# Attention backward on one core: query-major exponentials 384 keys wide, the fourth key tile by DMA transposes

## The chip, the cores and the metric

The kernel runs on one core of a Trainium2 chip. A core has TensorE (PE; its weight loads are listed as PEld), VectorE (DVE), ScalarE (ACT), GpSimd (POOL) and SyncE (SP), which here only issues DMAs. The metric is device time in microseconds, the median of three runs.

## The reference, cut to what matters

A layer of two branches, forward and backward. Branch A is attention over 2048 tokens with 32 heads of width 18; branch B is a long convolution with a state-space kernel; a gate mixes them. The stage in question is the attention with its gradients:

```python
qkv = (x @ wqkv).reshape(B, S, 3, H, Dh)          # S = 2048, D = 576, H = 32, Dh = 18
scores = einsum("bhqd,bhkd->bhqk", q, k) * Dh ** -0.5
p = softmax(scores, axis=-1)
o = einsum("bhqk,bhkd->bhqd", p, v)
a = o.reshape(B, S, D) @ wo
# and the gradients: dv = p^T do, ds = p * (do v^T - rowsum(do * o)), dq = ds k, dk = ds^T q
out = g * a + (1 - g) * b                          # with jax.vjp of the whole for grad_out
```

## The kernel before, in words

Four heads form a group; there are 8 groups (NG). A unit is one group and one block of 512 queries (b), so there are 32 units (NU), and each is worked in 32 steps (NST). All engines' work is written out by hand in one loop over the global step G, in the order in which each engine runs it; nothing is reordered afterwards, and the waits between engines are put in from the tiles' uses. The backward half of a unit runs OFF = 39 steps behind its forward half, so in steps 39 to 1023 both halves run, of neighbouring units.

What one step does, in this order on TensorE:

- P1: a pair of score matmuls of two heads, key-major (128 keys of tile i by 512 queries), into a PSUM tile `ps_P`. ScalarE takes the exponential into a stored tile `PT` (128 x 1024, bf16, L1388), out of a ring of 41 such tiles. `PT` is kept until the backward half of the unit uses it.
- a burst of the slot of this step: dV, dQ or dK, each in two halves (`dv_half`, `dq_half`, `dk_half`), or transposes by TensorE (`turn_p`). All share one PSUM buffer (`accB`), which DVE evicts (L1151, L1169, L1188, L1102). A key block (kq) of 512 keys takes eight steps.
- P3: the same scores once more for the backward half, query-major (128 queries of tile ii by 512 keys), with a second exponential into `eb` (L1393). dV needs the probabilities with the queries on the partitions, since a matmul sums over partitions. The key-major `PT` is what the forward output and ds need.
- P2: two matmuls of dO and V with two PSUM buffers, from which DVE makes ds by multiplying with `PT` (L1398).
- in half of the steps, the forward output `accO` from `PT`.

Scores thus are exponentiated twice, once in each layout. P1 and P3 use two score buffers in turn, P2 two of its own.

dK needs ds with keys and queries exchanged (`dsT`). Three of the four heads of a tile of ds are turned by a DMA transpose, issued on SP as soon as DVE has made them (L1406), the fourth by TensorE; two pairs of tiles in a unit are done otherwise (`by_pe`). SP also issues, in program order, the loads of the next pieces (`QaT`, `KaT`, `VaT`, and by DMA transposes `Vtok`, `Ktok`, `Qtok`) and the transposes of finished gradients (`gT`). When a group ends, eight `gT` for dK and dV and four `Ktok` and four `VaT` of the next group come within about one unit: this is called a change of group below; there are seven in the stretch where both halves run.

At the end of a unit's forward half, `post_forward` evicts `accO` (DVE, `oT`), turns it on TensorE, takes reciprocals (`rl`, DVE), and POOL multiplies: `dOa` from `rl` (L1049) and `prod` from it (L1051), which DVE then reduces (L1057). POOL's other work during attention is the basis of branch B (L506, stored by L559), written between the steps at an even rate (`e_emit`), and packing of gradients (`dtk`, L1075, stored by L1076). POOL also works strictly in the order written.

After the last step the next stage (branch B) begins; its first loads are issued on SP during the last 39 steps, in which only the backward half runs.

Line numbers here and in the profile are those of the kernel before; the same code lies some lines further down in the kernel after (L1406 becomes L1427, L1010 becomes L1012, L1071 becomes L1073).

## Time and profile before

| what | value |
|---|---|
| median of 3 runs | 2677.37 us (2671.75 to 2682.45) |
| span of the profiled execution | 2673.6 us |
| TensorE clock granted, mean | 0.968 |
| busy over the span: PE, DVE, ACT, POOL | 90%, 86%, 88%, 68% |
| exponentials, key-major (L1388) | x1024, record 1075 ns each |
| exponentials, query-major (L1393) | x1024, record 1070 ns each |
| products ds (L1398) | x2048, record 683 ns each |
| DMA transposes of ds (L1406) | x512 |
| queue q1 (SP) | 1108346 packets, 339.13 MB |

The profiled execution is given by its span alone, which lies 3.8 us under the median of the runs. The attention stage reaches from the first score matmul at 120.6 us to the last product at 2086.6 us. A record of an instruction on ScalarE or DVE is longer than its distance to the next one, since neighbours overlap; the pace is read from start to start. The DMA share is the sum of packet times over 16 engines and can exceed 1.

### The profile page before, as it was taken

What the parts mean: (1) busy time and instruction counts of PE and PEld (TensorE: products, weight loads), DVE (VectorE), ACT (ScalarE), POOL (GpSimd) and SP (SyncE); (2) the same over time, 40 slices, a digit from 0 to 9 for tenths busy, and PEclk for the clock granted to TensorE, in tenths of its full rate; (3) what the DMA queues carried; (4) which work ended last, traced back from release to release, by engine and by line L of the source; (5) the groups of instructions that cost most, each with busy time, mean ns of one, the idle gap of its engine ahead of it and who ended that gap; (6) DMA issues with size and microseconds to landing.
All of it is one profiled execution on the core that took longest, in us unless ns stands there. A gap on an engine that the chain in (4) does not pass through costs nothing.

```text
span 2673.6 us, 69952 instructions
## 1 busy us (share of the span) xinstructions
PE 2405.5 (90%) x27411; PEld 1134.6 (42%) x27411; DVE 2294.7 (86%) x4090; ACT 2352.0 (88%) x2744; POOL 1830.1 (68%) x2845
## 2 busy tenths in 40 slices
PE   8999999998889898889898999989988699999999
PEld 4433333333333333333333333333232489998756
DVE  5748999999889999889899999999897499999964
ACT  5589999999999999999999999999996489999321
POOL 0388878888888888888878888887931135555431
PEclk9989999999999999999999999999896699999999
DMA  7747889879979978997898899779668979998996
GB/s 232 202 114 152 150 171 177 162 156 181 169 151 172 185 157 163 173 167 152 165 179 157 157 172 169 154 164 181 134 136 174 224 229 262 260 263 250 269 255 136
DMA packets 1155478, 486.63 MB, mean 182 GB/s; under 512 B 1071062, under 2 KB 1108551, under 8 KB 1152843
## 3 DMA queue, kind: packets, MB, share of 16 engines
q1 hardware_dynamic: 1108346, 339.13, 64.3%
q0 software_dynamic: 44784, 137.52, 19.2%
q10 hardware_dynamic: 2016, 5.51, 0.7%
q8 instruction: 214, 3.51, 0.6%
q14 instruction: 118, 0.96, 0.1%
HBM read 146.27 MB, written 93.80 MB: 90 GB/s over the span
## 4 chain that ended last, share of the span: by engine, by line
ACT 39%; PE 28%; DVE 22%; issue 6%; DMA 3%; POOL 2%; SPq 1%; ACTq 0%; DVEq 0%; POOLq 0%
ACT eb L1393 23%; ACT PT L1388 14%; PE ps_P L30 8%; DVE ds L1398 7%; DVE tz L733 3%; DVE wab L753 3%; PE accV L30 2%; PE ps_dx L30 2%; PE turn_p L1097 2%; DVE tz L736 2%; PE accK L30 2%; DVE HG L738 2%; PE yp L30 2%; DVE Rw L758 1%; DVE dvacc L1151 1%
## 5 line engine op out<-in xcount | busy, mean ns | idle before, releaser
L1398 DVE TENSOR_TENSOR ds<-ps_P,PT 128x512 bf16<-128x512 f32 x2048 | 1312.5, 683 | 127.8 <-PE ps_P L30 87.3
L1393 ACT ACTIVATE eb<-ps_P 128x1024 bf16<-128x1024 f32 x1024 | 1095.7, 1070 | 44.3 <-PE ps_P L30 44.2
L1388 ACT ACTIVATE PT<-ps_P 128x1024 bf16<-128x1024 f32 x1024 | 1099.6, 1075 | 11.0 <-PE ps_P L30 9.5
L30 PE MATMUL ps_P<-dOaT,VaT_g 32*128 32x512 bf16 x2048 | 583.1, 390 | 30.8 <-DVE ds L1398 15.4
L506 POOL TENSOR_TENSOR et<-eG,eT 128x448 f32<-128x448 f32 x576 | 542.9, 963 | 10.7
L30 PE MATMUL ps_P<-QaT_g,KaT_g 32*128 32x512 bf16 x2048 | 404.7, 387 | 126.6 <-ACT PT L1388 122.2
L30 PE MATMUL ps_P<-KaT_g,QaT_g 32*128 32x512 bf16 x2048 | 408.9, 392 | 2.0 <-ACT eb L1393 1.4
L506 POOL TENSOR_TENSOR Eo<-et,et 128x448 bf16<-128x448 f32 x288 | 327.2, 1136 | 20.8
L30 PEld LDWEIGHTS <-KaT_g 32*128 32x128 bf16 x2048 | 147.4, 91 | 456.1 <-issue 438.2
L30 PEld LDWEIGHTS <-QaT_g 32*128 32x128 bf16 x2048 | 115.7, 91 | 288.6 <-issue 266.7
L30 PE MATMUL accV<-eb,dOa 128*32 128x512 bf16 x2048 | 185.6, 396 | 26.8 <-ACT eb L1393 26.5
L30 PE MATMUL accO<-PT,Vtok_g 128*32 128x512 bf16 x2048 | 207.9, 395 | 0.1
L30 PE MATMUL accK<-dsT,Qtok_g 128*32 128x256 bf16 x4096 | 165.3, 283 | 21.3 <-DMA dsT<-ds 19.9
L30 PE MATMUL accQ<-ds,Ktok_g 128*32 128x512 bf16 x2048 | 161.9, 394 | 2.2 <-DVE dvacc L1151 1.9
L30 PEld LDWEIGHTS <-Vtok_g 128*32 128x32 bf16 x2048 | 52.8, 93 | 222.6 <-issue 222.6
L1102 DVE COPY dsT<-turn_p 128x1024 bf16<-128x1024 bf16 (+1 forms) x216 | 139.2, 644 | 3.4 <-PE turn_p L1097 3.4
L1097 PE MATMUL turn_p<-ident_bf,ds 128*128 128x128 bf16 x1664 | 136.2, 225 | 1.4 <-DVE gb L1169 0.8
L672 ACT COPY E1e<-etp 128x1024 bf16<-128x1024 bf16 x132 | 125.4, 1063 | 2.7 <-PE etp L671 2.7
L30 PEld LDWEIGHTS <-Qtok_g 128*32 128x32 bf16 x4096 | 88.6, 97 | 87.8 <-issue 57.9
L506 POOL TENSOR_TENSOR et<-eT 128x32 f32<-128x32 f32 (+3 forms) x288 | 116.2, 424 | 11.4
L1097 PEld LDWEIGHTS <-ds 128*128 128x128 bf16 x1664 | 98.9, 100 | 50.2 <-issue 50.0
L1075 POOL COPY dtk<-gT 128x288 bf16<-128x288 bf16 x96 | 40.9, 426 | 107.6 <-DMA dqkv_d<-dtk 47.2
(295 smaller groups left out, 3731.0 us busy)
## 6 DMA issues: line engine op xcount, KB each, us to landing
E_d<-Eo POOLq DMA_DIRECT2D x144, 256.0 KB, 3.3
E1n<-E_d POOLq DMA_DIRECT2D x30, 1024.0 KB, 6.6
T0w<-Kp_d SPq DMA_DIRECT2D x18, 1024.0 KB
xs<-xb_d POOLq DMA_DIRECT2D x28, 512.0 KB, 9.9
dsT<-ds SPq DMA_TRANSPOSE x512
dqkv_d<-dtk POOLq DMA_DIRECT2D x96, 72.0 KB, 4.3
Md_d<-mst SPq DMA_DIRECT2D x18, 288.0 KB
skw<-Md_d SPq DMA_DIRECT2D x72, 64.0 KB
```

Of the source, the lines that this page charges most:

```text
L30: return nc.tensor.matmul(out, lhsT=lhsT, rhs=rhs, start=start, stop=stop, **kw)
L506: nc.gpsimd.tensor_tensor(out, a, b, op=op)
L672: copy(E_[:, 4 * q:4 * q + 4], pt_)
L733: nc.vector.tensor_tensor(tz[x], HG[:, :, k - 1].unsqueeze(1).to_broadcast([P, 2, 2, n, CB]), ZZ.unsqueeze(3).to_broadcast([P, 2, 2, n, CB ...
L736: nc.vector.tensor_tensor(tz[x][:, 0], tz[x][:, 0], UVk[:, :, :, k, :], op=A.add)
L738: nc.vector.tensor_tensor(HG[:, :, k], tz[x][:, 0], tz[x][:, 1, ::-1], op=A.add)
L753: nc.vector.tensor_tensor(wab, h_, w_, op=A.mult)
L1097: nc.tensor.transpose(pt_[:, x, qb, :], t_[:, qb * P:(qb + 1) * P], ident_bf)
L1102: (nc.scalar.copy if NTOT <= now[0] < NTOT + OFF else nc.vector.tensor_copy)(o_(), pt_[:, x:x + n])
L1388: nc.scalar.activation(U["PT"][i, j // 2], ps, ACT.Exp)
L1393: nc.scalar.activation(e, ps, ACT.Exp)
L1398: nc.vector.tensor_tensor(U["ds"][i][:, j, :], ps, U["PT"][i, j // 2][:, j % 2, :], op=A.mult)
```

## The change

Query-major scores and exponentials now cover only the first 384 keys of each block of 512 (KT = KB - P). For the fourth key tile of each block, the stored key-major tiles `PT` of both head pairs are turned by a DMA transpose on SP into `PTt` (two buffers), and dV of these 128 keys is made from `PTt`: in each half burst, eight matmuls of 384 columns and eight of 128 in place of eight of 512. The transposes of a block are issued one and two steps after the block's first backward step, five or six steps ahead of its dV burst. The `eb` tiles shrink to 2 x 384; the number of all other tiles stays.

```diff
-        woT = [eds.tile([P, 2, 512], BF, tag="eb", bufs=8, name="eb")...
-        dO_st = [eds.tile([P, 2, 512], BF, tag="eb", bufs=8, name="eb") for _ in range(3)]
+        woT = [eds.tile([P, 2, 384], BF, tag="eb", bufs=8, name="eb")...
+        dO_st = [eds.tile([P, 2, 384], BF, tag="eb", bufs=8, name="eb") for _ in range(3)]
...
+            KT = KB - P
+            TURNED = (0, 1)
...
+                def turn_p(u, kq, pair):
+                    U = UN[u]
+                    t_ = U["PTt", kq, pair] = work.tile([P, 2 * TPQ, P], BF, tag="PTt", bufs=2, name="PTt")
+                    nc.sync.dma_start_transpose(out=t_, in_=U["PT"][kq * TPQ + 3, pair].rearrange("p x q -> p (x q)"))
...
                 def dv_half(g, b, kq, h, acc):
                     U = UN[(g, b)]
-                    for ii in (2 * h, 2 * h + 1):
+
+                    def stored(ii):
                         for j in range(4):
-                            mm(acc[HP * j:HP * (j + 1), :], lhsT=U["dOa"][:, ii, j, :], rhs=U["eb"].pop((kq, ii, j)),
+                            mm(acc[HP * j:HP * (j + 1), 0:KT], lhsT=U["dOa"][:, ii, j, :], rhs=U["eb"].pop((kq, ii, j)),
                                start=(ii == 0), stop=(ii == 3), tile_position=(0, HP * j))
+
+                    def turned(ii):
+                        for j in range(4):
+                            mm(acc[HP * j:HP * (j + 1), KT:KB], lhsT=U["dOa"][:, ii, j, :], rhs=U["PTt", kq, j // 2][:, j % 2 * TPQ + ii, :],
+                               start=False, stop=False, tile_position=(0, HP * j))
+                    stored(2 * h)
+                    turned(2 * h)
+                    turned(2 * h + 1)
+                    stored(2 * h + 1)
...
+                for u_ in range(NU):
+                    for kq_ in range(NQ):
+                        for x_, pair_ in enumerate(TURNED):
+                            at(("pre", u_ * NST + OFF + 8 * kq_ + 1 + x_), lambda u_=u_, kq_=kq_, pair_=pair_: turn_p(units[u_], kq_, pair_))
...
-                            row(ps[:, x, :], T["QaT", b][:, ii * P:(ii + 1) * P], T["KaT", kq], jo + x)
+                            row(ps[:, x, 0:KT], T["QaT", b][:, ii * P:(ii + 1) * P], T["KaT", kq][:, 0:KT], jo + x)
...
-                            e = eds.tile([P, 2, KB], BF, tag="eb", bufs=8, name="eb")
+                            e = eds.tile([P, 2, KT], BF, tag="eb", bufs=8, name="eb")
...
-                            nc.scalar.activation(e, ps, ACT.Exp)
+                            nc.scalar.activation(e, ps[:, :, 0:KT], ACT.Exp)
```

Instructions issued on SP rise by the 256 transposes (two for each of 4 key blocks of 32 units), those of TensorE by 2048 matmuls with their weight loads; ScalarE, DVE and POOL issue the same ones as before.

More of the change, by code (lines that the diff above doesn't have):

```diff
@@ L125, in build @@
         d_aT = [eds.tile([P, 4, 512], BF, tag="ds", bufs=5, name="ds") for _ in range(DC)]
-        woT = [eds.tile([P, 2, 512], BF, tag="eb", bufs=8, name="eb").rearrange("p a b -> p (a b)")[:, 0:D] for _ in range(DC)]
-        dO_st = [eds.tile([P, 2, 512], BF, tag="eb", bufs=8, name="eb") for _ in range(3)]
+        woT = [eds.tile([P, 2, 384], BF, tag="eb", bufs=8, name="eb").rearrange("p a b -> p (a b)")[:, 0:D] for _ in range(DC)]
+        dO_st = [eds.tile([P, 2, 384], BF, tag="eb", bufs=8, name="eb") for _ in range(3)]
         with ExitStack() as ctx:
```

## Prediction

> **What bounds the kernel now.** I read the page's busy shares and 40 slices first, then stretches of equal length inside the attention stage, then the timeline engine by engine. The page says that three engines are nearly full over the span, and POOL not far behind:

> ```profile
> PE 2405.5 (90%) x27411; PEld 1134.6 (42%) x27411; DVE 2294.7 (86%) x4090; ACT 2352.0 (88%) x2744; POOL 1830.1 (68%) x2845
> ```

> Key-major and query-major scores run side by side in 985 of the 1024 steps, from 172 to 2000 us. Two stretches of 59 us there, about one unit (32 steps) each, the second at a change of head group:

> ```profile
> core 0: us, PE busy (x) PEld busy (x) DVE busy (x) ACT busy (x) POOL busy (x), PEclk, DMA share, GB/s
> 1259.00:1318.00 59.00, 53.12 (x580) 18.56 (x576) 53.45 (x90) 59.00 (x66) 49.83 (x78) 1.00 0.78 154
> 1318.00:1377.00 59.00, 53.37 (x580) 18.66 (x577) 53.55 (x89) 59.00 (x66) 47.25 (x78) 1.00 1.03 185
> ```

> The columns are busy us and instructions of PE, PEld, DVE, ACT and POOL, then clock, DMA share, GB/s. ACT is busy all 59.00 us of both, so ScalarE sets the pace. The DMA share goes from 0.78 to 1.03 between them and the pace does not move: that share, above 1, is no ceiling.

> ScalarE's records overlap, so the pace is read from start to start:

> ```profile
> 1008.92 1.07 ACT L1388 ACTIVATE PT<-ps_P 128x1024 bf16<-128x1024 f32 x1
> 1009.83 1.08 ACT L1393 ACTIVATE eb<-ps_P 128x1024 bf16<-128x1024 f32 x1
> 1010.73 1.09 ACT L1388 ACTIVATE PT<-ps_P 128x1024 bf16<-128x1024 f32 x1
> 2167.66 2.10 ACT L708 ACTIVATE UV<-uvp 128x512 bf16<-128x512 f32 x4
> 2169.59 1.06 ACT L743 CAST gR<-HG 128x960 bf16<-128x960 f32 x1
> ```

> A 128x1024 exponential costs 0.905 us (1008.92 to 1010.73 is two), not the 1.07 of its record. Four 128x512 ones cost 1.93, so 0.483 each. Between them lies 0.824 ns per column.

> What the other engines have in hand is POOL's story. Once a unit POOL must turn `rl` into `dOa` and `prod` before DVE can go on (L1049, L1051), between basis operations that it does in the order they were written:

> ```profile
> POOL dOa L1049 <- DVE rl L1044: 92.4, 25, 8.3
> POOL dtk L1075 <- DMA dqkv_d<-dtk: 34.6, 18, 5.6
> 1293.08 0.68 POOL L1049 TENSOR_TENSOR dOa<-dO_b,rl 128x288 bf16<-128x288 bf16 x1 [4.91 <-DVE rl L1044]
> 1411.01 0.68 POOL L1049 TENSOR_TENSOR dOa<-dO_b,rl 128x288 bf16<-128x288 bf16 x1
> ```

> Those two rows are two units apart: 117.93 us, 58.97 a unit. At 1293 POOL had waited 4.91 us for DVE, so it had that much to spare; at 1411, behind a change of group, it had nothing. Over the stretch its spare time at this point is 92.4 us.

> **The change, part by part.** *Exponentials.* 256 columns fewer on each of 985 is 256 x 0.824 ns = 0.211 us a step, 208 us in all, if nothing else bound. A unit of ScalarE would fall to 32 x (0.905 + 0.694) = 51.2 us.

> *DVE* loses nothing:

> ```profile
> 1008.18 1.28 DVE L1398 TENSOR_TENSOR ds<-ps_P,PT 128x512 bf16<-128x512 f32 x2
> 1009.37 0.68 DVE L1102 COPY dsT<-turn_p 128x1024 bf16<-128x1024 bf16 x1
> 1009.97 1.28 DVE L1398 TENSOR_TENSOR ds<-ps_P,PT 128x512 bf16<-128x512 f32 x2
> ```

> From 1008.18 to 1009.37 are two products, 0.595 each; the 128x1024 copy behind takes 0.60. A unit has 64 products, 12 evictions (dV, dQ, dK per key block), some 6.5 such copies and `oT`, 83.5 at 0.60 = 50.1, and about 1.5 of small ones: 51.6 us. So DVE stands where ScalarE will: two engines at 51 to 52.

> *TensorE.* The score matmul of 384 columns runs beside the P2 pair of 512, so nothing is gained there. The dV burst gets 16 more matmuls per key block, with 16 weight loads. First half of one burst, TensorE, before and after (`eb`: query-major tiles, `PTt`: turned key-major ones):

> ```order
> L30 MATMUL accV_2128<-eb_1980,dOa0_1232 32x512
> ...
> L30 MATMUL accV_2128<-eb_1954,dOa0_1232 32x512
> ...
> L30 MATMUL accV_2128<-eb_2033,dOa0_1232 32x512
> ...
> L30 MATMUL accV_2128<-eb_2007,dOa0_1232 32x512
> ...
> L30 MATMUL ps_P3_2138<-KaT_g_1247,QaT_g_1245 128x512
> ```

> ```order
> L30 MATMUL accV_2132<-eb_1982,dOa0_1232 32x384
> ...
> L30 MATMUL accV_2132<-eb_1954,dOa0_1232 32x384
> ...
> L30 MATMUL accV_2132<-PTt_1964,dOa0_1232 32x128
> ...
> L30 MATMUL accV_2132<-PTt_1997,dOa0_1232 32x128
> ...
> L30 MATMUL accV_2132<-eb_2037,dOa0_1232 32x384
> ```

> The turned keys stand between the stored pieces; the columns in all are the same. Eight matmuls and sixteen with as many columns took

> ```profile
> 1001.46 0.62 PE L30 MATMUL accV<-eb,dOa 128*32 128x512 bf16 x8
> 1010.36 0.62 PE L30 MATMUL accK<-dsT,Qtok_g 128*32 128x256 bf16 x16
> L30 PE MATMUL ps_P<-QaT_g,KaT_g 32*128 32x512 bf16 x2048 | 404.7, 387 | 126.6 <-ACT PT L1388 122.2
> ```

> 0.62 both, so the extra instructions cost nothing that shows, and at most a tenth of that, 0.06 us a half, which two rows of equal length would still hide (I take 0). The cover is the third row: TensorE waits 122.2 us for ScalarE to free the score buffer. Were that gone, 0.06 x 246 halves = 15 us.

> *SP, the transposes.* 256 DMA transposes of 8x128 go onto the queue that already issues `dsT`, in order, each `dsT` waiting for DVE. Prices, min/median/max ns:

> ```profile
> L1406 SPq DMA_TRANSPOSE dsT<-ds x512: 1274/1458/5387, 175.8 to 2098.6; - x171
> L1010 SPq DMA_TRANSPOSE Ktok_g<-QKV_d x32: 1225/1262/2299, 158.9 to 1851.5; - x32
> ```

> `dsT` is 12x128 at 1.46, `Ktok` 4x128 at 1.26, so I put 8x128 between, at 1.36; the far end is 2.20 (below). The same place on SP at a change of head group:

> ```order
> L1406 DMA_TRANSPOSE dsT_24063<-ds_24028 128x12x128
> L1010 DMA_TRANSPOSE Qtok_g_24066<-QKV_d_72 128x4x128
> L1071 DMA_TRANSPOSE gT_24068<-dvacc_20631 128x4x128
> L1010 DMA_TRANSPOSE Ktok_g_24102<-QKV_d_72 128x4x128
> L1406 DMA_TRANSPOSE dsT_24063<-ds_24093 128x12x128
> ```

> ```order
> L1116 DMA_TRANSPOSE PTt_25595<-PT_24336 128x8x128
> L1427 DMA_TRANSPOSE dsT_25625<-ds_25588 128x12x128
> L1012 DMA_TRANSPOSE Qtok_g_25628<-QKV_d_72 128x4x128
> L1116 DMA_TRANSPOSE PTt_25630<-PT_24376 128x8x128
> L1073 DMA_TRANSPOSE gT_25632<-dvacc_21951 128x4x128
> L1012 DMA_TRANSPOSE Ktok_g_25666<-QKV_d_72 128x4x128
> L1427 DMA_TRANSPOSE dsT_25625<-ds_25657 128x12x128
> ```

> One `PTt` now stands ahead of the first `dsT`, one ahead of the second. Each waits on SP for the dV burst that frees its buffer, a step earlier; behind it stands a `dsT` whose products come later still, so that wait costs nothing. dV itself wants the `PTt` five or six steps (9 us) after issue. In the trace of before that place reads

> ```profile
> 1329.04 2.20 SPq L1071 DMA_TRANSPOSE gT<-dkacc  x1
> 1331.34 4.13 SPq L1406 DMA_TRANSPOSE dsT<-ds  x2
> 1335.52 1.26 SPq L1010 DMA_TRANSPOSE Qtok_g<-QKV_d  x1
> 1336.89 1.31 SPq L1071 DMA_TRANSPOSE gT<-dvacc  x1
> 1338.25 1.27 SPq L1010 DMA_TRANSPOSE Ktok_g<-QKV_d  x1
> 1339.62 4.58 SPq L1406 DMA_TRANSPOSE dsT<-ds  x2
> ...
> 1346.26 6.12 SPq L1406 DMA_TRANSPOSE dsT<-ds  x2
> ```

> Each row starts where the last ends; SP idles only inside the pairs of `dsT`, 4.13 - 2.92 and 4.58 - 2.92, 2.9 us in the 14.92 of a key block. Two `PTt` take 2.8. So SP is just full there and a unit at a change of group stays at 4 x 14.92 = 59.7. In the other 24 units SP issues 16 x 1.46 + 8 x 1.36 + 3 x 1.26 and some 4 us of plain loads and gaps, 42 us: hidden.

> What a late `dsT` does, the trace has once:

> ```profile
> 1132.01 1.05 PE L30 MATMUL accK<-dsT,Qtok_g 128*32 128x256 bf16 x16 [1.85 <-DMA dsT<-ds]
> 1133.63 1.02 ACT L1393 ACTIVATE eb<-ps_P 128x1024 bf16<-128x1024 f32 x1 [2.14 <-PE ps_P L30]
> 1000.00:1100.00 100.00, 90.05 (x975) 31.14 (x971) 90.11 (x149) 100.00 (x109) 89.18 (x148) 1.00 0.86 163
> 1100.00:1200.00 100.00, 89.05 (x950) 30.91 (x949) 87.99 (x146) 97.12 (x106) 80.95 (x124) 0.97 0.98 173
> ```

> dK waited 1.85 us, ScalarE 2.14, and the clock fell (0.97 over 100 us). ScalarE did 106 instructions instead of 109.5: 3.5 x 0.905 = 3.2 us lost. [...]

> *The tail*, 2000 to 2116, where no exponential bounds. SP is solid there and `dsT` dear, and the stage behind waits for SP's last load:

> ```profile
> 2068.41 2.98 SPq L1406 DMA_TRANSPOSE dsT<-ds  x1
> 2088.01 4.24 SPq L1406 DMA_TRANSPOSE dsT<-ds  x1
> 2103.55 1.12 ACT L603 ACTIVATE RX<-RXn,l1col 128x480 bf16<-128x480 bf16 x1 [16.64 <-DMA E1n<-E_d]
> ```

> Four `PTt` (last two key blocks) fall into it, 1.4 to 4 us each; at 2, since they are half the size of those rows, 8 us lost.

> *Sum.* POOL lets through at most its 92.4 us. 3 of them lie in the seven units at changes of group, which stay; its longest wait, 8.3, is where it runs out of work and DVE and ScalarE allow some 5. That leaves 86. SP takes 0.7 x 7 = 5 and, I take, three more stalls at 3.2 = 10; the tail 8. 86 - 5 - 10 - 8 = 63 of the profiled 2673.6: 2610.6. The median of the runs lies 3.8 above this span, so **2614**. An ordinary unit then takes 55.5 us, all from POOL's spare time, and ScalarE idles 3 to 4 us in it.

> **Rivals.** *POOL gives way.* If its late `dOa` only eats the step or so that DVE leaves before the reduction, ordinary units go to 53, a little above 51.6: 6 x 24 = 143, less 23: 2557. Against it: at 1411 POOL was already on time with nothing left.

> *The ring of P2 and product binds.* With no key-major work left, the query-major score pairs start at

> ```profile
> 2002.51 0.39 PE L30 MATMUL ps_P<-KaT_g,QaT_g 32*128 32x512 bf16 x2
> 2004.22 0.39 PE L30 MATMUL ps_P<-KaT_g,QaT_g 32*128 32x512 bf16 x2
> 2006.17 0.39 PE L30 MATMUL ps_P<-KaT_g,QaT_g 32*128 32x512 bf16 x2
> 2007.99 0.52 PE L30 MATMUL ps_P<-KaT_g,QaT_g 32*128 32x512 bf16 x2
> ```

> 1.71, 1.95 and 1.82 apart, mean 1.83, 58.5 us a unit: nothing saved but 0.5 x 31 = 15, less 23, so 2685, no change. Against it: these three steps hold `oT`, `rl` and `Ob` of a unit's end.

> *SP becomes the bound* (slower). If at changes of group a `dsT` right behind a `PTt` costs what `gT` cost at 1329, 2.20, and each `PTt` 1.9 (as far above its 1.36), the unit takes 16 x 2.2 + 8 x 1.9 + 13 x 1.26 + 6 = 72.8 us, 13.8 more, seven times 97; with 16 in the tail, 2673.6 - 86 + 97 + 16 + 3.8 = 2704. It turns slower where such a unit passes 58.97 + (86 - 8)/7 = 70. For it: stalls of this kind exist. Against: most `dsT` cost 1.46. That the DMA engines themselves fill I count here; against it speaks that they can move more:

> ```profile
> 1001.00:1002.00 1.00, 1.00 (x11) 0.22 (x9) 1.00 (x3) 1.00 (x2) 0.97 (x3) 1.00 1.23 283
> ```

> 283 GB/s while only transposes ran, against 154 and 185 above; 256 x 256 KB in 1.75 ms adds 38.

> **Chances.** Forecast 0.60, POOL gives way 0.14, ring 0.14, SP 0.12. The range reaches both outer rivals, 2557 and 2704: 2555 to 2705. A run tells about 0.5% (13 us). Faster is the forecast nearly whole and the first rival, 0.71; same 0.16; slower 0.13.

> **What would show it.** Right: exponentials of `eb` 0.69 apart, ScalarE idle in ordinary units, POOL's wait before `dOa` near 0, DVE waiting for `prod`, units at changes of group at 59 to 61 with `dsT` waits of TensorE. Wrong: ordinary units at 53 or 58, `dsT` issues above 2 us, half clock outside the stalls, or dV waiting for `PTt`.

## The result

The changed kernel is slower: 2746.42 us median (2732.61 to 2752.76, 4 runs) against 2676.62 (2671.75 to 2682.45, 4 runs), a ratio of 1.0249 with a 95% interval of 1.0208 to 1.0291. The profiled execution has a span of 2751.0 us, 77.4 more than the 2673.6 before. The forecast was 2614, and its range ended at 2705.

The page, where it answers to the rows of before: first the granted clock in 40 slices and the shares of the chain that ended last in the kernel before, then busy time of the engines, clock and chain in the changed kernel.

```profile
PEclk9989999999999999999999999999896699999999
ACT 39%; PE 28%; DVE 22%; issue 6%; DMA 3%; POOL 2%; SPq 1%; ACTq 0%; DVEq 0%; POOLq 0%
...
PE 2505.4 (91%) x29459; PEld 1181.9 (43%) x29459; DVE 2280.3 (83%) x4090; ACT 2200.9 (80%) x2744; POOL 1830.5 (67%) x2845
PEclk9999998897798798978989997998998599999999
PE 55%; DVE 25%; DMA 11%; ACT 4%; issue 3%; SPq 1%; POOL 0%; ACTq 0%; DVEq 0%; POOLq 0%
PE ps_P L30 20%; DVE ds L1419 11%; PE accV L30 7%; DMA PTt<-PT 6%; PE accK L30 5%; PE accQ L30 5%; PE accO L30 5%; DMA dsT<-ds 4%; DVE tz L733 2%; DVE wab L753 2%; PE ps_dx L30 2%; PE ps_proj L30 2%; DVE tz L736 2%; PE ps_dwq L30 1%; DVE HG
```

ScalarE went from 2352.0 us busy to 2200.9: the 151 us less of work are there. TensorE went from 2405.5 to 2505.4 although only narrow matmuls were added, and the clock row, full before in the attention stage up to its end, dips to 7 and 8 all along it. In the chain ScalarE fell from 39% to 4%; it now holds `PTt<-PT` with 6% and `dsT<-ds` with 4%.

A unit at a time tells more. In the attention stage, cut at every 32nd key-major exponential, the units 1 to 30 add up to 1781.8 us before and to 1854.2 after. An ordinary unit before, then two neighbouring units after, the second at a change of head group (columns as before: us, busy of PE, PEld, DVE, ACT, POOL, clock, DMA share, GB/s):

```profile
1190.00:1248.92 58.92, 53.03 (x576) 18.55 (x576) 53.37 (x89) 58.92 (x66) 49.87 (x82) 1.00 0.74 163
...
1320.03:1376.56 56.53, 53.09 (x648) 19.32 (x640) 52.70 (x89) 53.84 (x65) 49.68 (x79) 1.00 1.07 197
1376.56:1441.60 65.04, 60.60 (x648) 20.27 (x640) 53.17 (x89) 54.88 (x65) 51.04 (x84) 0.82 1.10 194
```

The undisturbed unit is 56.53 us, and seven of the 30 lie within 0.1 us of that; it was 58.92. The next one has the same numbers of instructions, but took 65.04, with TensorE busy 60.60 instead of 53.09 at a clock of 0.82. So the change has two effects that nearly hide each other in the total: 30 x (58.92 - 56.53) = 72 us gained, and 1854.2 - 30 x 56.53 = 158 us spent above the undisturbed pace, where before it was 14. The units at a change of group are 68.3 us on average, those right behind them 63.3, the rest 58.3.

What TensorE waited for in the stage after (us in all, times, longest):

```profile
PE accV L30 <- DMA PTt<-PT: 30.9, 27, 6.0
PE accK L30 <- DMA dsT<-ds: 26.4, 15, 4.7
```

dV and dK waited 57 us, in 42 waits; before, dK waited 2.1 us in two. (The expectations below speak of 74 us, with the 16.4 that weight loads waited for `dsT`; laid over dK's waits, all but 4.5 us of these are the same time.) The 57 us are two fifths of the 144 that were lost. The rest goes with the half clock, which follows such waits, but other gaps of TensorE too, as the run without transposes below shows (208 us of half clock, with 9.1 us of such waits). One wait, on SP and on TensorE:

```profile
400.64 1.39 SPq L1116 DMA_TRANSPOSE PTt<-PT  x1
402.12 1.56 SPq L1073 DMA_TRANSPOSE gT<-dvacc  x1
403.74 1.26 SPq L1012 DMA_TRANSPOSE Ktok_g<-QKV_d  x1
405.09 2.46 SPq L1427 DMA_TRANSPOSE dsT<-ds  x1
...
408.28 1.56 SPq L1427 DMA_TRANSPOSE dsT<-ds  x1
...
411.05 1.23 SPq L1073 DMA_TRANSPOSE gT<-dkacc  x1
412.37 2.86 SPq L1427 DMA_TRANSPOSE dsT<-ds  x1
...
416.91 0.39 PE L30 MATMUL ps_P<-QaT_g,KaT_g 32*128 32x512 bf16 x2
418.13 0.62 PE L30 MATMUL accK<-dsT,Qtok_g 128*32 128x256 bf16 x16 [0.83 <-DMA dsT<-ds]
...
421.25 0.63 PE L30 MATMUL ps_P<-QaT_g,KaT_g 32*128 32x512 bf16 x2
...
419.50:443.40 23.90, 23.56 (x200) 7.46 (x198) 16.40 (x26) 17.37 (x21) 18.00 (x38) 0.50 1.09 180
```

dK's wait names the two `dsT` issued at 408.28 and 412.37. By the trace the last product that the second needs ended at 406.60, but SP, still busy with what stands ahead, was through with its issue only at 415.22. dK then waits 0.83 us, and from 419.5 to 443.4 the granted clock is 0.50: two score matmuls that took 0.39 us take 0.63. In these 23.90 us ScalarE did 21 instructions; at the undisturbed pace (65 in 56.53) it would have done 27.5. The 6.5 missing ones are 5.6 us lost behind a wait of 0.83.

### The profile page after: what moved, and what is told of

Read it like the earlier page. It is cut to its first block, busy times and chain, and to the rows that moved or that the text cites. A ratio compares the mean times of both kernels' runs of the same rounds, so it can differ in the third digit from the quotient of the medians.

```text
span 2751.0 us, 74632 instructions
## 1 busy us (share of the span) xinstructions
PE 2505.4 (91%) x29459; PEld 1181.9 (43%) x29459; DVE 2280.3 (83%) x4090; ACT 2200.9 (80%) x2744; POOL 1830.5 (67%) x2845
## 4 chain that ended last, share of the span: by engine, by line
PE 55%; DVE 25%; DMA 11%; ACT 4%; issue 3%; SPq 1%; POOL 0%; ACTq 0%; DVEq 0%; POOLq 0%
PE ps_P L30 20%; DVE ds L1419 11%; PE accV L30 7%; DMA PTt<-PT 6%; PE accK L30 5%; PE accQ L30 5%; PE accO L30 5%; DMA dsT<-ds 4%; DVE tz L733 2%; DVE wab L753 2%; PE ps_dx L30 2%; PE ps_proj L30 2%; DVE tz L736 2%; PE ps_dwq L30 1%; DVE HG L738 1%
## 5 line engine op out<-in xcount | busy, mean ns | idle before, releaser
L1419 DVE TENSOR_TENSOR ds<-ps_P,PT 128x512 bf16<-128x512 f32 x2048 | 1304.8, 683 | 177.3 <-PE ps_P L30 158.9
L1409 ACT ACTIVATE PT<-ps_P 128x1024 bf16<-128x1024 f32 x1024 | 1053.1, 1029 | 100.8 <-PE ps_P L30 80.8
L1414 ACT ACTIVATE eb<-ps_P 128x768 bf16<-128x768 f32 x1024 | 835.7, 816 | 179.3 <-PE ps_P L30 172.6
L30 PE MATMUL ps_P<-dOaT,VaT_g 32*128 32x512 bf16 x2048 | 647.3, 414 | 58.3 <-DVE ds L1419 45.9
L30 PE MATMUL ps_P<-QaT_g,KaT_g 32*128 32x512 bf16 x2048 | 451.9, 414 | 25.9 <-ACT PT L1409 25.0
L30 PE MATMUL ps_P<-KaT_g,QaT_g 32*128 32x384 bf16 x2048 | 371.2, 359 | 1.2 <-ACT PT L1409 0.5
L30 PEld LDWEIGHTS <-KaT_g 32*128 32x128 bf16 x2048 | 130.3, 92 | 328.6 <-issue 304.4
L30 PE MATMUL accO<-PT,Vtok_g 128*32 128x512 bf16 x2048 | 222.0, 423 | 0.1
L30 PE MATMUL accK<-dsT,Qtok_g 128*32 128x256 bf16 x4096 | 177.5, 299 | 47.9 <-DMA dsT<-ds 44.4
L30 PEld LDWEIGHTS <-QaT_g 32*128 32x128 bf16 x2048 | 98.3, 92 | 282.3 <-issue 263.3
L30 PE MATMUL accV<-eb,dOa 128*32 128x384 bf16 x2048 | 189.8, 366 | 6.8 <-ACT eb L1414 6.3
L30 PE MATMUL accQ<-ds,Ktok_g 128*32 128x512 bf16 x2048 | 175.3, 423 | 1.7 <-DVE dvacc L1168 1.7
L30 PEld LDWEIGHTS <-dOa 128*32 128x32 bf16 x4096 | 88.1, 100 | 182.0 <-issue 165.7
L30 PEld LDWEIGHTS <-Vtok_g 128*32 128x32 bf16 x2048 | 53.4, 94 | 258.8 <-issue 258.4
L30 PEld LDWEIGHTS <-Qtok_g 128*32 128x32 bf16 x4096 | 99.6, 101 | 127.5 <-issue 80.0
```

What stands on the lines that cost most here:

```text
L30: return nc.tensor.matmul(out, lhsT=lhsT, rhs=rhs, start=start, stop=stop, **kw)
L1409: nc.scalar.activation(U["PT"][i, j // 2], ps, ACT.Exp)
L1414: nc.scalar.activation(e, ps[:, :, 0:KT], ACT.Exp)
L1419: nc.vector.tensor_tensor(U["ds"][i][:, j, :], ps, U["PT"][i, j // 2][:, j % 2, :], op=A.mult)
```

## The experiments

Kernels with one run are told by the span of that run; the changed kernel's own four runs lie 20 us apart, so a difference of single runs under some 20 us shows nothing by itself. Spans of the two kernels for comparison: 2673.6 before, 2751.0 changed. Where it helps, the sum of units 1 to 30 is given too, since it leaves out what differs ahead of and behind the stage.

**Without transposes and turned matmuls.**

```diff
-            TURNED = (0, 1)
+            TURNED = ()
...
-                    turned(2 * h)
-                    turned(2 * h + 1)
```

> The changed kernel without the transposes of the stored tiles and without the turned matmuls that read them (the last 128 keys of each key block are left out of dV); the exponentials stay 384 wide. Theory A (TensorE paces the undisturbed unit at 56.5 us, and late transposes with the half clock behind them cost the rest): the stalls go, and the undisturbed unit is what TensorE needs without the extra matmuls, about 58.9 - 122.2/31 = 55.0 us; total 2673.6 - 31 x 3.9 + 3.8, about 2555. Rival POOL (basis work paces): 55.5 us in ordinary units with no wait of POOL before dOa, total about 2575. Rival ring (score pair and product pace, whatever the matmuls): 56.5 as now, total about 2600. Rival ScalarE and VectorE alone: 52 us, total about 2460.

2658.3 us. The undisturbed unit is 56.10, as the ring had it, a little lower:

```profile
1723.40:1779.50 56.10, 52.43 (x584) 17.99 (x576) 52.71 (x89) 53.71 (x65) 49.92 (x78) 1.00 0.83 165
by line: DVE ds L1417 31.0%; PE ps_P L30 25.1%; PE accK L30 8.0%; PE accQ L30 7.5%; PE accO L30 6.5%; PE accV L30 5.4%; issue 5.2%; DVE dsT L1104 4.0%; DVE dkacc L1203 2.4%; DVE dqa L1184 1.8%; DVE Ob L1049 0.8%; DVE oT L1037 0.8%; DVE dOaT
```

The chain through this unit is no one engine's, and ScalarE is not in it: products (VectorE 31%) and score matmuls (TensorE 25%) take turns, with the matmuls of dK, dQ, the forward output and dV between them. In this order of work, narrowing the exponentials therefore offers 2.8 us a unit, 85 in all. Of that, 69 us went again into units above 56.10, with 208 us of half clock in them, though dK waited for `dsT` only 9.1 us in all. So theory A had the undisturbed unit and the total wrong.

**The turned matmuls alone**, on two tiles written once:

```diff
-                    t_ = U["PTt", kq, pair] = work.tile([P, 2 * TPQ, P], BF, tag="PTt", bufs=2, name="PTt")
-                    nc.sync.dma_start_transpose(out=t_, in_=U["PT"][kq * TPQ + 3, pair].rearrange("p x q -> p (x q)"))
+                    U["PTt", kq, pair] = ptt_fix[pair]
```

> The changed kernel with the turned matmuls kept, but reading two tiles written once before the stage (zeros), so that no transpose of a stored tile is issued (the last 128 keys of dV are left out). Theory A: TensorE's work is that of the changed kernel, so every unit is 56.5 us, the stalls are gone, no half clock inside the stage to speak of; total 2673.6 - 31 x 2.4 + 3.8, about 2603. The difference to the run without the turned matmuls is their price: 1.5 us a unit by theory A, 0 by the prediction's step that they cost nothing. Rival (the stalls are not the transposes' doing): 2740 as the changed kernel.

2633.4 us, the fastest of all, with units of 56.55. The matmuls cost 0.45 us in an undisturbed unit, 14 us in all. Yet the run is 25 us shorter than the one without them (18 of these in units 1 to 30), with 85 us of half clock instead of 208. That work on TensorE which fills its gaps paid for itself here is a reading of one run each, little above their scatter.

**The transposes alone**, read by nobody:

```diff
-                    turned(2 * h)
-                    turned(2 * h + 1)
```

> The changed kernel with the transposes of the stored tiles issued as before, but nothing reads what they write (no turned matmuls; the last 128 keys of dV are left out). Theory A1 (the stalls come from SP's queue being full, so dsT is late too): units at a change of head group still 60 to 68 us with waits of dK for dsT and half clock; total about 2555 + 8 x 9 = 2630. Theory A2 (only dV's own wait for the turned tile stalls): as without the transposes, about 2555. Rival (the transfers slow everything by filling the DMA engines): all units longer alike, ordinary ones above 57, total above 2680.

2738.7 us, 80.4 more than without them. The undisturbed units stay at 56.10 (the 256 transposes do not slow them), those at changes of group are 67.2 on average, and dK waits:

```profile
PE accK L30 <- DMA dsT<-ds: 63.4, 25, 5.4
1418.70:1486.62 67.92, 63.23 (x584) 19.94 (x576) 53.47 (x89) 55.09 (x65) 49.01 (x77) 0.72 1.03 179
```

Theory A1 has it, and nearly its price (75 us over the kernel without transposes, which itself lay 100 us above its forecast). As nothing reads the tiles here, no `PTt` can hold SP up by waiting for a dV burst, so that is not the cause. From before to the changed kernel the spans thus go by -15 (narrower exponentials), +80 (256 transposes) and +12 (their readers), units 1 to 30 by -30, +79 and +23. Only the middle step is well above the scatter of single runs.

**Which part of the load.** The same without a reader, each transpose cut to an eighth, and one of double size, read from device memory, instead of two:

```diff
-                    nc.sync.dma_start_transpose(out=t_, in_=U["PT"][kq * TPQ + 3, pair].rearrange("p x q -> p (x q)"))
+                    nc.sync.dma_start_transpose(out=t_[:, 0:1, :], in_=U["PT"][kq * TPQ + 3, pair].rearrange("p x q -> p (x q)")[:, 0:P])
```

```diff
-            TURNED = (0, 1)
+            TURNED = (0,)
...
+                    nc.sync.dma_start_transpose(out=t_, in_=QKV_d[ROW0["K"] + 4 * u[0] * WID["K"]:ROW0["K"] + 4 * u[0] * WID["K"] + P, 0:S])
```

> As the run whose turned tiles nobody reads (the last 128 keys of dV are left out), with each of the 256 transposes cut from 8x128 to 1x128: as many issues on SP, an eighth of the bytes. Theory I (SP's issue time, some 1.25 us whatever the size, makes dsT late): about 2740, as with the full transposes. Theory B (the transposes fill the DMA engines): about 2660, as without them. An issue that itself shrinks below 1 us would leave it in between.

> The other half of that pair: one transpose of 16x128 per key block instead of two of 8x128, read from device memory and read by nobody (the last 128 keys of dV are left out): as many bytes through the transposing queue, half the issues on SP. Theory B: about 2740, as with two. Theory I: 2690 to 2705, if an issue of 16x128 takes some 1.5 us instead of 2 x 1.28; between 2660 and 2710.

2693.9 us (35.6 above the kernel without transposes) and 2726.7 (68.4 above). SP's time for the added issues and for `dsT`, min/median/max ns, of the first, the second, and the full transposes:

```profile
L1116 SPq DMA_TRANSPOSE PTt<-PT x256: 1120/1184/2649, 183.9 to 2103.0; - x128
L1425 SPq DMA_TRANSPOSE dsT<-ds x512: 1274/1530/6760, 189.2 to 2118.5; - x171
L1116 SPq DMA_TRANSPOSE PTt<-QKV_d x128: 1409/2595/8834, 176.2 to 2125.6; - x128
L1116 SPq DMA_TRANSPOSE PTt<-PT x256: 1231/1313/4251, 177.6 to 2141.7; - x128
L1425 SPq DMA_TRANSPOSE dsT<-ds x512: 1273/1668/6370, 182.4 to 2157.8; - x171
```

An issue of 1x128 holds SP 1.18 us, nearly as long as one of 8x128 (1.31), and costs nearly half as much in the end (36 of 80 us): neither theory, both parts. The other run does not cross it as meant, since an issue of 16x128 took 2.60 us, so that halving the issues did not halve SP's time. It only shows that the loss goes with SP time and bytes together.

The traces tell where the lateness arises. With each `dsT` paired to the last product that it needs, its issue can be late (from the end of that product to the end of the issue; 1.30 us at the least) or its transfer slow (from the start of the issue to its landing). Medians in us:

| kernel | issue, changes of group | issue, units behind | transfer, changes of group |
|---|---|---|---|
| before | 3.0 | 1.6 | 4.4 |
| no transposes | 3.8 | 1.6 | 4.8 |
| 1x128, no reader | 6.5 | 2.3 | 4.8 |
| 8x128, no reader | 8.1 | 3.4 | 5.0 |
| changed | 7.2 | 3.4 | 5.3 |

Most of it lies on SP's queue: the issue comes off it 4 us later than before, the transfer takes 1 us more.

**Without the dummy matmul.**

```diff
-            NFILL = {"V": 1, "Q": 0, "K": 0}
+            NFILL = {"V": 0, "Q": 0, "K": 0}
```

> The changed kernel without the one dummy matmul of 512 columns ahead of each dV burst (8 in a unit, 0.37 us each); the result is the reference's. Theory A: TensorE paces the undisturbed unit, which falls from 56.5 by 8 x 0.34 to about 53.8; the stalls at changes of group stay or grow, since SP has less time for as many transposes; total 2746 - 0.6 x 31 x 2.7 = 2700, between 2660 and 2740. Rival POOL: undisturbed units stop at 55.5, total 2715 or more. Rival ring: 56.5 stays, total 2746.

2746.52 us median, ratio to before 1.0278 (1.0217 to 1.0339): as the changed kernel. With 2.7 us of matmuls a unit gone, the undisturbed unit fell by 0.8, to 55.74, and the total did not follow (389 us of half clock instead of 375). TensorE alone does not pace that unit; POOL doesn't either, since it still waits for VectorE in two units of 55.74:

```profile
POOL dOa L1051 <- DVE rl L1046: 3.2, 2, 1.8
```

**One pair turned**, and that without the dummy matmul:

```diff
-            TURNED = (0, 1)
+            TURNED = (0,)
...
-                            e = eds.tile([P, 2, KT], BF, tag="eb", bufs=8, name="eb")
+                            w_ = KT if j == 0 else KB
+                            e = eds.tile([P, 2, w_], BF, tag="eb" if j == 0 else "ebw", bufs=4, name="eb")
```

> The changed kernel with only the first of the two head pairs turned: its exponentials are 384 keys wide, those of the second pair stay 512, and there are 128 transposes instead of 256; the result is the reference's. ScalarE's unit is then about 16 x (0.905 + 0.694) + 16 x 1.81 = 54.5 us, below the 56.1 at which the undisturbed unit stood without any turning, so nothing of the ordinary unit's gain is lost: 56.3 us. What is left of the stalls decides. Theory S (the extra transposes cost in proportion): halfway between the run without them and the changed kernel, 2700. Theory F (they cost only where they overfill a unit at a change of group): 2660 to 2680, no slower than before. Rival (any narrowing of ScalarE's work brings the stalls, the transposes matter little): 2660, as without turning.

> The one-pair kernel without the dummy matmul ahead of each dV burst; the result is the reference's. Undisturbed units fall from 56.9 to about 56.3 (0.8 less is what the same edit gave with both pairs turned); total 2667 - 0.6 x 31 = 2650 if the stalls stay, 2667 if they take it back, as they did with both pairs turned.

2667.30 us, ratio to before 0.9944 (0.9912 to 0.9975), and 2658.41, ratio 0.9914 (0.9883 to 0.9946). Both are faster than the changed kernel, and by 0.6% and 0.9% than the one before: clear of noise, but small. Their intervals overlap, so the two are not told apart. In the first the undisturbed unit is 56.94, 0.4 over that with both pairs, and of the waits for a turned tile 2.1 us are left, all of weight loads. The waits for `dsT` are as long as in the changed kernel, but half clock is 78 us instead of 375:

```profile
1202.30:1259.24 56.94, 53.51 (x611) 19.39 (x608) 53.21 (x89) 56.52 (x65) 49.75 (x91) 1.00 0.94 172
PE accK L30 <- DMA dsT<-ds: 25.6, 16, 5.0
PEld L30 <- DMA dsT<-ds: 24.9, 23, 5.3
```

**Fewer loads at changes of group.**

```diff
+                    if g and nm in ("Ktok", "Vtok"):
+                        grp_t.setdefault(g, {})[nm, m] = grp_t[0][nm, m]
+                        return
```

> The changed kernel in which the token-major K and V tiles of the first head group are kept for all groups (their 8 transposes from memory at each of the seven changes of group are left out, so the later groups' gradients and outputs are made with wrong tiles). Theory L (stalls come where these loads, the gradients' transposes and the two new transposes per key block pile up on SP): the units at changes of group fall from 68 us on average to about 60, those behind them from 63 to 60; total 2751 - 7 x (8 + 3) = 2675. Rival (the stalls come from elsewhere, as the transposed gradients or the basis traffic): 2735 or more.

2707.6 us, between the two theories. The units at changes of group fall from 68.3 to 63.6 us, those behind from 63.3 to 61.6, and the waits of dK for `dsT` from 26.4 to 11.4 us, while dV's waits for the turned tiles stay (34.4). A `dsT` at a change of group comes off SP 4.9 us after its product instead of 7.2. The pile-up on SP is a cause: of what such a unit takes above 56.53, two fifths come with these loads.

**The old pace.** Whether the transposes would have stayed hidden at 58.9 us a unit, as the prediction held, took three tries. Two slow ScalarE with a second exponential:

```diff
                             nc.scalar.activation(e, ps[:, :, 0:KT], ACT.Exp)
+                            nc.scalar.activation(e[:, :, 0:108], ps[:, :, 0:108], ACT.Exp)
```

```diff
                             nc.scalar.activation(e, ps[:, :, 0:KT], ACT.Exp)
+                            nc.scalar.activation(ps[:, :, KT:KT + 100], ps[:, :, 0:100], ACT.Exp)
```

> The changed kernel with ScalarE slowed to the pace of the kernel before: behind each 384-wide exponential it does the first 108 columns of it again, to the same place, about 0.24 us (1.84 us a step, 58.8 us a unit); the result is the reference's. All transposes and turned matmuls are there. Theory P (the transposes hurt because the units are shorter, so that dsT and the turned tiles have less time and TensorE no slack to catch up): few stalls, 2680 to 2700. Theory L (the load hurts at any pace): the stalls of the changed kernel, some 140 us, come on top of the old pace, 2780 or more.

> A second try at the old pace: behind each 384-wide exponential ScalarE does one of 2 x 100 columns into the part of the score buffer that nobody reads, so that it waits for nothing of its own (the first try waited for the first exponential's end and made a step of 2.00 us, with the clock halved by TensorE's idle time). About 0.23 us, 1.83 us a step, 58.5 us a unit; the result is the reference's. Theory P (late transposes hurt because the units are shorter): waits for the turned tiles and dsT as few as in the first try, under 10 us in all, total 2670 to 2700. Theory L (the load hurts at any pace): waits of 50 us or more, total 2750 or more. If the units come out above 60 us, idle time and half clock decide again, and only the waits tell.

> The control to that: the same extra exponentials in the kernel without the transposes and turned matmuls (the last 128 keys of dV are left out). Units of 58.5 us, no stalls: 2665, near the kernel before. If it is as slow as the one with transposes, the two differ by nothing and the pace alone decides.

3001.2, 2912.2 and 2950.5 us: all missed their pace. The added exponential waits for the end of the one before it in both forms, so a step took 2.0 us:

```profile
301.21 0.82 ACT L1414 ACTIVATE eb<-ps_P 128x768 bf16<-128x768 f32 x1
302.06 0.35 ACT L1415 ACTIVATE eb<-ps_P 128x216 bf16<-128x216 f32 x1
302.31 1.02 ACT L1409 ACTIVATE PT<-ps_P 128x1024 bf16<-128x1024 f32 x1
...
343.15:411.86 68.71, 59.72 (x643) 22.14 (x643) 54.06 (x89) 64.63 (x97) 50.92 (x96) 0.80 0.83 166
```

At 64 us a unit and more TensorE stands idle for 9 of the 68.71 us shown, and the clock halves with hardly a stall: it is 0.80 in the unit shown, where the waits for `dsT` and the turned tiles come to 0.2 us. The three runs have 974, 561 and 913 us of half clock. The run without transposes has 0.2 us of waits for `dsT`, and is slower than the one with them. So the spans say little on the load. The waits do: up to 2000 us the three rows that make 74 us in the changed kernel make 7 in the first run, and in the second 15:

```profile
PE accV L30 <- DMA PTt<-PT: 7.3, 5, 3.1
PE accK L30 <- DMA dsT<-ds: 4.3, 5, 1.6
PEld L30 <- DMA dsT<-ds: 3.0, 6, 1.9
```

At this pace the load is nearly hidden.

The third splits the exponentials instead, the key-major one in four and the query-major one in two, with and without the transposes:

```diff
-                            nc.scalar.activation(U["PT"][i, j // 2], ps, ACT.Exp)
+                            for x in range(2):
+                                for y in range(2):
+                                    nc.scalar.activation(U["PT"][i, j // 2][:, x, y * 256:(y + 1) * 256], ps[:, x, y * 256:(y + 1) * 256], ACT.Exp)
```

> Third try at the old pace, now with nothing added: the changed kernel's exponentials are split, the key-major one in four of 256 columns, the query-major one in two of 384. From 0.905 us for 1024 columns and 0.483 for 512, an exponential of n costs 0.061 + 0.000824 n, so a step takes 4 x 0.272 + 2 x 0.377 = 1.84 us, 59.0 us a unit, if the pieces run as close as whole ones did; the result is the reference's. Theory P (late transposes hurt because the units are shorter): waits for dsT and the turned tiles under 25 us in all, against 74 in the changed kernel; total 2670 to 2710. Theory L (the load hurts at any pace): waits of 50 us or more, total 2750 to 2820.

> Its control: the same split exponentials without transposes and turned matmuls (the last 128 keys of dV are left out). 2665 to 2685, near the kernel before, if TensorE's idle time is as there; if half clock fills it as in the two runs at 64 us and more, the pace of before itself is not reached and only the waits can be compared.

2824.0 and 2760.8 us. The shortest units are 59.9 with and without, 1.0 over the old pace, and the two differ by the transposes and their readers alone: 63 us in the spans, 53 in units 1 to 30. The waits up to 2000 us, first with, then without:

```profile
PE accV L30 <- DMA PTt<-PT: 22.4, 13, 5.6
PE accK L30 <- DMA dsT<-ds: 15.2, 12, 3.3
PEld L30 <- DMA dsT<-ds: 5.0, 7, 1.6
```

```profile
PE accK L30 <- DMA dsT<-ds: 0.2, 1, 0.2
PEld L30 <- DMA dsT<-ds: 2.0, 7, 0.4
```

43 us of waits against 2, units at changes of group of 68.2 us against 61.7. That is nearer to theory L, which asked for 50 and 2750 or more, than to P, with 25 and 2710 at most. The same step costs 93 us at the new pace (102 in units 1 to 30). So half to two thirds of the loss is there at 60 us a unit already, where the prediction held the transposes hidden; the waits then shrink with the pace, from 74 us at 56.5 over 43 at 60 to 15 and 7 above 64. Neither theory is whole, and each point is one run. Both runs are dearer than forecast, in good part because the control itself has 311 us of half clock at 60 us a unit.

## Why the prediction was wrong

- *What ScalarE offers*: right. The narrow exponentials follow at 0.69 us, the wide ones at 0.90, and ScalarE is busy 53.84 us of an undisturbed unit.

```profile
1341.93 0.81 ACT L1414 ACTIVATE eb<-ps_P 128x768 bf16<-128x768 f32 x1
1342.62 1.03 ACT L1409 ACTIVATE PT<-ps_P 128x1024 bf16<-128x1024 f32 x1
1343.52 0.83 ACT L1414 ACTIVATE eb<-ps_P 128x768 bf16<-128x768 f32 x1
```

- *TensorE's extra matmuls*: the cover is nearly gone (122.2 us of waits fell to 25.0), and the price that the prediction gave for that case, 15 us, is what the fixed tiles showed (0.45 x 31 = 14). It was put at 0 in the sum.
- *POOL's 86 us*: the wrong bound, with nearly the right size. The ordinary unit was forecast at 55.5 and is 56.53. It is held by products and matmuls taking turns, not by POOL, which waits for VectorE once in each such unit (below, two of them). The ring rival came nearest to that, but at 58.5 us a unit, because its three steps held a unit's end, and without the bursts that are part of the turn.

```profile
POOL dOa L1051 <- DVE rl L1046: 7.7, 2, 5.1
```

- *SP at changes of group*: this step failed. I summed the issue times, found SP "just full" and so put the units at 59.7 and the extra stalls at three. This queue, in order and just full, passed each delay on: a `dsT` at a change of group came off it 7.2 us after its product instead of 3.0, in the next unit 3.4 instead of 1.6. Those units are 68.3 us, and the next ones, called hidden with 42 us of issues, are 63.3. In place of 5 + 10 us stand 158 - 14 = 144. The run without transposes is 69 us above its undisturbed pace too, which comes with the shorter units and not with the queue's load; the transposes and their readers make up the rest.
- *A stall's price*, 3.2 us: mis-sized. A single row of before gave it, with a clock of 0.97 over 100 us; after, a wait of 0.83 us cost 5.6, and there are 42 waits of dV and dK. The 375 us of half clock in units 1 to 30, at the 0.39 us that a unit lengthens for each, are 146 us, nearly the whole loss (the waits themselves lie within that slope). That is how the two go together from unit to unit; it does not show that each wait caused the half clock behind it.
- *SP as the bound*, the slower rival: closest. It had 72.8 us for the units at changes of group and turned slower at 70. The measured 68.3 are below that point; the total is slower all the same, because the units behind them are hit too, which none of my cases held.
- *The tail*: from the end of unit 30 to the first instruction of ScalarE that the next stage's load held up 135.3 us against 130.5, 4.8 dearer; 8 was forecast.

The sum as measured: -72 + 144 + 5 = 77.

## What to carry over

Before work is put on an in-order queue that is nearly full in some stretches, do not count those stretches as hidden: the delay is passed to the instructions behind, here into the next unit too (63.3 us, against 58.3 in the rest). Find the pace at which the next limit closes (here 56.1 us, where products and matmuls take turns) and take off the bounding engine only as much as that; turning one pair instead of two kept the undisturbed unit within 0.4 us, and it halved the load that was added to the queue. Where the trace shows half clock behind short waits, price a wait by that half clock and not by its own length.

## What the hardware did that I had not expected

More work on TensorE went with a shorter time in two pairs of runs: 2633.4 us with the turned matmuls on fixed tiles against 2658.3 without any (half clock 85 and 208 us), and, at 64 us a unit and more, 2912.2 with transposes and turned matmuls against 2950.5 without (561 and 913). Each is one run, and taking the dummy matmul out did not lengthen a kernel, so this is not shown as a rule.

On ScalarE, an exponential followed by one that takes the same columns of the score buffer again lost its overlap: 0.85 us instead of 0.69 from its start to the next. The pieces of one split exponential, on columns of their own, kept theirs: four of 256 columns in 1.08 us. The runs do not show what makes the difference.
